# A fused mLSTM attention and gated FFN on one core: the first attention product moved to head pairs on two row groups, with split loads and a new order

## The chip, the cores and the metric

One core of a Trainium2 chip runs the whole program in one launch. The metric is the device time of one execution in microseconds (us), lower is better. The profile takes a single execution and gives its span, from the first to the last instruction it records.

## The reference

The input is q, k, v and an output gate of shape 4 x 8 x 768 x 40 (batch, heads, sequence, head size) with two gates per head and token. Attention is a recurrence with a stabilised exponential decay; its result, 320 wide per token, goes through a feed-forward network (FFN) with a convolution of three taps along the sequence.

```python
for t in range(S):
    m_new = np.maximum(f_gate[:, :, t] + m, i_gate[:, :, t])
    f_stab, i_stab = np.exp(f_gate[:, :, t] + m - m_new), np.exp(i_gate[:, :, t] - m_new)
    C = f_stab * C + i_stab * outer(vt, kt)
    n = f_stab * n + i_stab * kt
    y[:, :, t] = sigmoid(o_gate) * (C @ qt) / max(abs(n . qt), 1)
h = np.maximum(x @ w_in, 0)                  # 320 -> 1024
conv_out = sum(conv_w[k] * shifted(h, k) for k in range(3))
out = (h * sigmoid(conv_out)) @ w_out        # 1024 -> 320
```

## The kernel before, in words

**Tiles.** The sequence is cut into chunks of 128 tokens: 6 to a sequence, 24 in all, written s. Two neighbouring chunks make a unit u of 256 tokens (12 units); the FFN works on units, in eight blocks f of 128 hidden columns, which are treated in four pairs p.

**Attention of a chunk.** The gates are scanned on 32 rows (batch times head), and the decays reach the 128 rows of a chunk in two ways: for the first NP = 3 chunks by products on PE (ch_gpe, L402 to L409: a 512 column product with the triangle and four with a 32 row operand, columns of the identity against the 32 rows of Gt), later by a DMA that repeats rows of a DRAM tile (ch_loadw, L418), with a mask on POOL (L432) and an exponential on ACT (L439). The first product, S = k q for eight heads (ch_s, L455 to L466), comes in two jobs s0 and s1 of four heads. Its operands have 120 or 80 rows, three heads deep: kz holds each head's k in its own 40 rows with zeros in the rest, and q has the three heads stacked. DVE multiplies S by the decays (ch_p, L471). The product with v (ch_pv, L491) adds to the part that comes from the running state (ch_inter, L482). The state Cst is advanced by ch_u on PE and ch_state on DVE (L513, L515), and its masked copy cb for the next chunk's ch_inter is made by two products on POOL or DVE (ch_cb, L521 and L522). DVE then divides (ch_rden, then ch_num at L547, which reads pY in PSUM and writes x in SBUF), applies the output gate (ch_x, L554), and PE transposes (ch_t, L575) into X, split into a high and a low part.

**FFN of a unit.** Block f: eight products into ph (f_m1, L618), a relu on ACT (L628), the taps on ACT (L636) and DVE (L650). A pair of blocks then has a tanh on ACT (L654), a product on DVE (L658), and a split into gh on ACT (L213) and gl on POOL (L209). The second FFN product (f_m2, L681) is one job of six products per block: gh with both parts of w_out and gl with the high part, for two halves k of the tokens. Weights arrive as 64 bit numbers and are converted by integer operations on DVE (L330 to L343) and a split on ACT and POOL.

**Order.** All work is a table of jobs (`at`, L703) with engine costs (COST), the jobs each waits for, and a tie breaker z (OFF). A planner (`order`, L86) places them when the program is built, and each engine runs its instructions in that fixed order. Buffers are rings (BUFS): pY has one buffer, freed by the job num; the PSUM tag m has three. Where the planner sees a gap on PE ahead of the first m1, it puts in `warm` products on zeros (L358). In the trace an fp32 product shows as two MATMUL rows, an fp32r product (ph, po, the triangle, the transposes) as one.

## Time and profile before

| | |
|---|---|
| median of 3 runs | 345.4 us (345.09 to 349.81) |
| the profiled execution, device time | 344.72 us |
| its span | 342.6 us |
| PE, DVE, ACT, POOL busy | 328.7, 262.9, 236.3, 202.7 us |
| moved by DMA | 46.09 MB |

PE is TensorE's products and PEld its weight loads, which overlap them; DVE, ACT and POOL are VectorE, ScalarE and GpSimd; SP issues the DMAs. A busy share counts products that overlap only once, and the mean duration of a PE row contains the time that it takes to drain, so what a row of products costs is read from start to start. PEclk, the granted clock, is in tenths of full speed.

### The profile page before, as it was taken

The page shows a single profiled execution, that of the slowest core. Times are in us where ns is not written, and L with a number is a line of the kernel's source. Part 1 is how long each engine was busy: PE and PEld are TensorE (multiplying, and loading weights), DVE is VectorE, ACT ScalarE, POOL GpSimd, SP SyncE. Part 2 cuts the span into 40 slices and gives each one's busy share as a digit, 9 for nine tenths or more (in the row PEclk, how much of TensorE's full clock was granted, in tenths as well). Part 3 has the DMA queues.
Part 4 walks back from the last instruction along what each step waited for, and adds up shares of the span by engine and source line. Part 5 has one row for each costly group of instructions (what it writes and reads, how often), then busy time and mean ns, then how long its engine had stood idle before and what let it go on. Part 6 is the DMA issues. An engine that isn't in the chain of part 4 may idle for free.

```text
span 342.6 us, 7422 instructions
## 1 busy us (share of the span) xinstructions
PE 328.7 (96%) x2534; PEld 322.3 (94%) x2534; DVE 262.9 (77%) x598; ACT 236.3 (69%) x610; POOL 202.7 (59%) x310
## 2 busy tenths in 40 slices
PE   7699898998999999999999999999999999999995
PEld 7588898999999999999999999999999999999995
DVE  4897889999998987778489877676888768566750
ACT  2355747879988668896958786769685536577871
POOL 7369898869968647584745661746563234343341
PEclk9855599999999999999999999999999999999999
DMA  6887658686717466174315452654211001010111
GB/s 167 273 250 299 215 196 271 192 256 180 221 53 219 150 194 205 64 216 157 101 58 153 127 160 93 187 182 147 94 59 41 0 2 38 2 38 2 38 41 38
DMA packets 18575, 46.09 MB, mean 135 GB/s; under 512 B 2579, under 2 KB 6347, under 8 KB 18539
## 3 DMA queue, kind: packets, MB, share of 16 engines
q1 hardware_dynamic: 18068, 45.22, 42.4%
q8 instruction: 20, 0.33, 0.5%
q10 hardware_dynamic: 471, 0.41, 0.4%
q14 instruction: 16, 0.13, 0.1%
HBM read 41.49 MB, written 4.13 MB: 133 GB/s over the span
## 4 chain that ended last, share of the span: by engine, by line
PE 71%; DVE 11%; POOL 6%; ACT 4%; DMA 3%; issue 3%; SPq 0%; POOLq 0%; DVEq 0%; ACTq 0%
PE po L681 22%; PE ph L618 22%; PE pY L491 10%; PE pS L464 9%; PE pY L482 3%; PE pU L502 3%; PE pT L575 2%; DMA wraw<-in_w_in 1%; DVE cv L650 1%; DVE ph L650 1%; ACT w L439 1%; DMA w<-G_d 1%; PE pg L408 1%; POOL gl L209 1%; POOL w L432 1%
## 5 line engine op out<-in xcount | busy, mean ns | idle before, releaser
L209 POOL TENSOR_TENSOR gl<-cv,gh 128x512 fp32r<-128x512 f32 x48 | 62.5, 1302 | 47.4 <-ACT gh L213 40.7
L618 PE MATMUL ph<-X,wi_h 128*128 128x258 f32 x480 | 77.1, 290 | 2.2 <-DVE cv L650 1.5
L618 PEld LDWEIGHTS ph<-X,wi_h 128*128 128x128 f32 x480 | 64.6, 190 | 3.0 <-ACT ph L636 1.7
L681 PE MATMUL po<-wo_h,gh 128*128 128x320 f32 x192 | 61.5, 320 | 0.5 <-ACT ot L687 0.5
L439 ACT ACTIVATE w<-w,aT 128x128 f32<-128x128 f32 x168 | 55.1, 391 | 8.1 <-POOL w L432 8.1
L650 DVE SCALAR_TENSOR_TENSOR ph<-h,cw_sb,ph 128x256 f32<-128x256 f32 x96 | 46.1, 483 | 18.9 <-ACT ph L636 18.4
L681 PE MATMUL po<-wo_l,gh 128*128 128x320 f32 x192 | 59.3, 309 | 0.0
L681 PE MATMUL po<-wo_h,gl 128*128 128x320 f32 x192 | 59.3, 309 | 0.0
L464 PE MATMUL pS<-q,kz 120*128 120x128 f32 (+1 forms) x384 | 53.1, 287 | 4.2 <-DVE aT L306 3.1
L464 PEld LDWEIGHTS pS<-q,kz 120*128 120x128 f32 (+1 forms) x384 | 48.6, 199 | 4.6 <-DVE aT L306 3.2
L658 DVE SCALAR_TENSOR_TENSOR cv<-cv,h 128x512 f32<-128x512 f32 x48 | 40.4, 844 | 15.9 <-ACT cv L654 15.6
L628 ACT ACTIVATE h<-ph 128x258 f32<-128x258 f32 x96 | 36.5, 380 | 23.1 <-PE ph L618 21.2
L650 DVE SCALAR_TENSOR_TENSOR cv<-h,cw_sb,ph 128x256 f32<-128x256 f32 x96 | 45.1, 476 | 8.1 <-POOL gl L209 4.9
L618 PE MATMUL ph<-X,wi_l 128*128 128x258 f32 x288 | 50.3, 283 | 0.0
L491 PE MATMUL pY<-n,w 128*128 128x41 f32 x384 | 47.8, 282 | 0.0
L491 PEld LDWEIGHTS pY<-n,w 128*128 128x128 f32 x384 | 47.2, 197 | 0.2
L636 ACT ACTIVATE ph<-h,cw_sb 128x256 f32<-128x256 f32 x96 | 45.6, 475 | 1.9
L654 ACT ACTIVATE cv<-cv 128x512 f32<-128x512 f32 x48 | 30.1, 627 | 16.3 <-DVE cv L650 9.3
L618 PEld LDWEIGHTS ph<-X,wi_l 128*128 128x128 f32 x288 | 41.3, 190 | 0.0
L213 ACT ACTIVATE gh<-cv 128x512 fp32r<-128x512 f32 x48 | 30.0, 624 | 11.2 <-PE po L681 11.2
L681 PEld LDWEIGHTS po<-wo_h,gh 128*128 128x128 f32 x192 | 36.2, 188 | 0.7 <-ACT ot L687 0.7
L681 PEld LDWEIGHTS po<-wo_l,gh 128*128 128x128 f32 x192 | 36.2, 189 | 0.0
(84 smaller groups left out, 530.0 us busy)
## 6 DMA issues: line engine op xcount, KB each, us to landing
n<-in_nat SPq DMA_DIRECT2D x24, 484.0 KB
w<-G_d SPq DMA_DIRECT2D x21, 512.0 KB
q<-in_qT SPq DMA_DIRECT2D x12, 360.0 KB
out<-ot SPq DMA_DIRECT2D x24, 160.0 KB
wraw<-in_w_in SPq DMA_DIRECT2D x8, 384.0 KB
kz<-in_kT SPq DMA_DIRECT2D x24, 120.0 KB
eq<-E_d SPq DMA_DIRECT2D x24, 120.0 KB
wraw<-in_w_out SPq DMA_DIRECT2D x8, 320.0 KB
```

What stands on the lines that cost most here:

```text
L209: (nc.gpsimd if e == "POOL" else nc.vector).tensor_tensor(out=out, in0=in0, in1=in1, op=op)
L213: nc.scalar.activation(out, in_, AF.Copy)
L439: nc.scalar.activation(w[:, h, :], g, AF.Exp, bias=aT[:, c, b * 8 + h : b * 8 + h + 1])
L464: nc.tensor.matmul(pS[:, j, :], lhsT=lhsT, rhs=rhs, start=(j == 0), stop=(j == 3), skip_group_check=True)
L491: nc.tensor.matmul(pY[:, h * VW : (h + 1) * VW], lhsT=r["w"][:, n, :], rhs=v[:, DM + h * VW : DM + (h + 1) * VW], start=(c == 0 and n == 0 ...
L618: nc.tensor.matmul(ph, lhsT=a, rhs=b_, start=(i == 0), stop=(i == len(mm) - 1))
L628: nc.scalar.activation(hj, ph, AF.Relu)
L636: nc.scalar.activation(c, hk, AF.Copy, scale=wk)
L650: nc.vector.scalar_tensor_tensor(o, hk, wk, c, op0=ALU.mult, op1=ALU.add)
L654: nc.scalar.activation(cv, cv, AF.Tanh, scale=0.5)
L658: nc.vector.scalar_tensor_tensor(cv, cv, 1.0, h[:, :, 1 : 1 + UT], op0=ALU.add, op1=ALU.mult)
L681: nc.tensor.matmul(obuf[u][k], lhsT=a, rhs=b_, start=(f == 0 and i == 0), stop=(f == 7 and i == 2))
```

## The change

- **S in pairs.** ch_s becomes one job per chunk: eight products of 40 rows, which alternate between rows 0 to 39 and rows 64 to 103, each of the two into a bank of its own (two PSUM buffers of tag m at once). kz with its zeros goes away; k2 and q2 hold four heads side by side in each row group.
- **Loads.** k2 and q2 come by four DMAs of 40 rows per unit (kP, qP), with three buffers; the stacked q (still needed for the state's product) is a job of its own, ldq. Per unit 327,680 bytes more are moved.
- **Decays.** Gt becomes the first 32 rows of Gz, 128 rows with zeros below, and the products of ch_gpe use all 128 rows. The gates are scanned in four groups (1, 1, 2, 2 chunks) where there were three (1, 1, 4).
- **State copy.** ch_cb is three ACT instructions with a row scale; POOL and DVE have none of it. The mask shrinks to 120 x 3.
- **Division.** ch_num works in place in PSUM; ch_x reads PSUM, writes x, and now frees pY.
- **Second FFN product.** m2 (gh, four products) waits for gh; a new job m2l (gl, two products) waits for gl. The output copy and its DMA are a job for each half.
- **Order.** New OFF, COST and planner constants, and a table FIX that sets z and a release time for many jobs one by one. The warm products in the program go from 22 to 92.

```diff
-GS = ((0, 1), (1, 2), (2, 6))
+GS = ((0, 1), (1, 2), (2, 4), (4, 6))
...
-    wk={"POOL": 0.97, "DVE": 0.55}, u={"PE": 0.6}, state={"DVE": 0.72}, cb={"POOL": 1.0, "DVE": 0.5}, s0={"PE": 0.86}, s1={"PE": 0.86}, p0={"DVE": 0.61}, p1={"DVE": 0.61},
+    wk={"POOL": 0.97, "DVE": 0.55}, u={"PE": 0.6}, state={"DVE": 0.72}, cb={"ACT": 0.85}, s={"PE": 1.15}, p0={"DVE": 0.61}, p1={"DVE": 0.61},
...
+FIX = dict(
+    g0={0: (3413.08, 0)},
...
-ACT_W = dict(pv0=0.3, pv1=0.3, gpe=0.4)
-WARM = (6.0, 60.0, 16)
+ACT_W = dict(pv0=0.3, pv1=0.3, s=0.5, ta0=0.3, ta1=0.3, ta2=0.3, ta3=0.3, tw0=0.3, tw1=0.3, tw2=0.3, tw3=0.3)
+WARM = (5.0, 60.0, 9, 1.8, 0.22)
...
-    Gt = const.tile([32, S], F32, name="Gt")
+    Gz = const.tile([P, S], F32, name="Gz")
+    nc.vector.memset(Gz[32:64, :], 0.0)
+    nc.vector.memset(Gz[64:P, :], 0.0)
+    Gt = Gz[0:32, :]
...
-    def att_kz(u):
-        q = sb.tile([120, 3 * UT], F32, name="q", tag="q", bufs=3)
+    def att_kq(u):
+        r = units.setdefault(u, {})
+        for nm, src in (("k2", kP), ("q2", qP)):
+            r[nm] = t = sb.tile([104, 4 * UT], F32, name=nm, tag=nm, bufs=3)
+            for k in range(2):
+                nc.sync.dma_start(out=t[64 * k : 64 * k + D, :], in_=src[u, k * D : k * D + D, :])
+
+    def att_q(u):
+        q = units.setdefault(u, {})["q"] = sb.tile([120, 3 * UT], F32, name="q", tag="q", bufs=3)
         nc.sync.dma_start(out=q, in_=qT[u])
...
-            nc.tensor.matmul(p[:, j, :], lhsT=id_sb[0:32, r : r + 1].to_broadcast([32, P]), rhs=Gt[:, c * P : (c + 1) * P],
+            nc.tensor.matmul(p[:, j, :], lhsT=id_sb[:, r : r + 1].to_broadcast([P, P]), rhs=Gz[:, c * P : (c + 1) * P],
...
-    def ch_s(s, half):
+    def ch_s(s):
         u, tt = s // 2, (s % 2) * P
         r, ur = chunks[s], units[u]
-        pS = ps_m.tile([P, 4, P], F32, name="pS", tag="m")
+        for half in range(2):
+            r["s", half] = ps_m.tile([P, 4, P], F32, name=f"pS{half}", tag="m")
         for j in range(4):
-            n = 4 * half + j
-            g = n % 3
-            kk = 40 * GRP[g][1]
-            lhsT, rhs = ur["kz"][0:kk, n, tt : tt + P], ur["q"][0:kk, g * UT + tt : g * UT + tt + P]
-            nc.tensor.matmul(pS[:, j, :], lhsT=lhsT, rhs=rhs,
-                             start=(j == 0), stop=(j == 3), skip_group_check=True)
-        r["s", half] = pS
+            for half in range(2):
+                k, q = (ur[x][64 * half : 64 * half + D, j * UT + tt : j * UT + tt + P] for x in ("k2", "q2"))
+                nc.tensor.matmul(r["s", half][:, j, :], lhsT=k, rhs=q, start=(j == 0), stop=(j == 3), skip_group_check=True)
...
-    def ch_cb(e, s):
+    def ch_cb(s):
         cb = sb.tile([120, 3, 123], F32, name="cb", tag="cb")
-        mk3 = mk_sb.rearrange("p (g v) -> p g v", g=3)
-        tt(e, cb[:, 0:2, :], Cst[:, 0:2, :], mk3[:, 0:2, :], ALU.mult)
-        tt(e, cb[0:80, 2, 0:82], Cst[0:80, 2, 0:82], mk3[0:80, 2, 0:82], ALU.mult)
+        for j in range(3):
+            ng, sl = 3 if j < 2 else 2, slice(j * VW, (j + 1) * VW)
+            nc.scalar.activation(cb[:, 0:ng, sl], Cst[:, 0:ng, sl], AF.Copy, scale=mk_sb[:, j : j + 1])
...
-        xf = sb.tile([P, 3 * P], F32, name="x", tag="x")
-        x = xf[:, 0:DM].rearrange("p (h d) -> p h d", h=H)
-        nc.vector.tensor_tensor(x, y3[:, :, 0:D], r["rd"].unsqueeze(2).to_broadcast([P, H, D]), op=ALU.mult)
-        r["x"] = xf
+        y3 = r["y"].rearrange("p (h d) -> p h d", h=H)[:, :, 0:D]
+        nc.vector.tensor_tensor(y3, y3, r["rd"].unsqueeze(2).to_broadcast([P, H, D]), op=ALU.mult)
 
     def ch_x(s):
         r = chunks[s]
-        xf = r["x"]
-        o = r["n"][:, DM + H * VW :]
-        nc.vector.scalar_tensor_tensor(xf[:, 0:DM], o, 1.0, xf[:, 0:DM], op0=ALU.add, op1=ALU.mult)
+        xf = r["x"] = sb.tile([P, 3 * P], F32, name="x", tag="x")
+        x, o = (t.rearrange("p (h d) -> p h d", h=H) for t in (xf[:, 0:DM], r["n"][:, DM + H * VW :]))
+        y3 = r["y"].rearrange("p (h d) -> p h d", h=H)[:, :, 0:D]
+        nc.vector.scalar_tensor_tensor(x, o, 1.0, y3, op0=ALU.add, op1=ALU.mult)
...
-        at("inter", z, qe + [("cb", us - 1)] if c else [], ch_inter, s, ring="y", users=[("num", s), ("rd1", s)], cost=0.63 if c else 0.01)
+        at("inter", z, qe + [("cb", us - 1)] if c else [], ch_inter, s, ring="y", users=[("x", s)], cost=0.63 if c else 0.01)
...
-    def f_m2(u, f):
+    def f_m2(u, f, low):
         p, j = f // 2, f % 2
-        gh, gl = gbuf[u, p]
-        if f == 0:
+        g = gbuf[u, p][low]
+        if f == 0 and not low:
             obuf[u] = [ps_o.tile([P, DM], F32, name=f"po{k}", tag=f"o{k}") for k in range(2)]
+        ws = [wo_h[:, f, :]] if low else [wo_h[:, f, :], wo_l[:, f, :]]
         for k in range(2):
-            ks = slice(k * P, (k + 1) * P)
-            mm = ((gh[:, j, ks], wo_h[:, f, :]), (gh[:, j, ks], wo_l[:, f, :]), (gl[:, j, ks], wo_h[:, f, :]))
-            for i, (a, b_) in enumerate(mm):
-                nc.tensor.matmul(obuf[u][k], lhsT=a, rhs=b_, start=(f == 0 and i == 0), stop=(f == 7 and i == 2))
-
-    def f_out(e, u):
-        for k in range(2):
-            ot = sb.tile([P, DM], F32, name="ot", tag="ot", bufs=2)
-            if e == "ACT":
-                nc.scalar.activation(ot, obuf[u][k], AF.Copy, scale=0.5)
-            else:
-                nc.vector.tensor_scalar(ot, obuf[u][k], 0.5, None, op0=ALU.mult)
-            ots[u, k] = ot
-        del obuf[u]
-
-    def f_outd(u):
-        b, t0 = u // 3, (u % 3) * UT
-        for k in range(2):
-            ot = ots.pop((u, k))
-            nc.sync.dma_start(out=out[b, t0 + k * P : t0 + (k + 1) * P, :], in_=ot)
+            for i, w in enumerate(ws):
+                nc.tensor.matmul(obuf[u][k], lhsT=g[:, j, k * P : (k + 1) * P], rhs=w, start=(f == 0 and not low and i == 0), stop=(f == 7 and low == 1))
...
-            at("m2", n, [("gl", 4 * u + f // 2), ("wsl", 8 + f)] + ([("m2", n - 1)] if n else [(f"exp", 4 * NP - 1)] if NP else []) + ([("out", u - 1)] if u and not f else []), f_m2, u, f)
+            at("m2", n, [("gh", 4 * u + f // 2), ("wsl", 8 + f)] + ([("m2", n - 1)] if n else [(f"exp", 4 * NP - 1)] if NP else []) + ([(f"out{k}", u - 1) for k in range(2)] if u and not f else []), f_m2, u, f, 0)
+            at("m2l", n, [("gl", 4 * u + f // 2), ("m2", n)] + ([("m2l", n - 1)] if n else []), f_m2, u, f, 1)
```

**The order on PE in the second half.** Rows of TensorE around one chunk's S, before (pU: the state's update; po: second FFN product; ph: first):

```order
L618 MATMUL ph<-X,wi_l 128x258 x3
L502 MATMUL pU<-n,wk 120x123 x2
L502 MATMUL pU<-n,wk 80x82
L464 MATMUL pS<-q,kz_108 128x128 x8
L681 MATMUL po_3283<-wo_h,gh 128x320
L681 MATMUL po_3283<-wo_l,gh 128x320
L681 MATMUL po_3283<-wo_h,gl 128x320
```

and at the like place now (k and q with numbers are the tiles k2 and q2, which the list shortens):

```order
L609 MATMUL pU<-n,wk 80x82
L785 MATMUL po_3233<-wo_h,gl 128x320
L785 MATMUL po_3234<-wo_h,gl 128x320
L572 MATMUL pS_3409<-q_2683,k_2680 128x128
L572 MATMUL pS_3410<-q_2683,k_2680 128x128
L572 MATMUL pS_3409<-q_2683,k_2680 128x128
L572 MATMUL pS_3410<-q_2683,k_2680 128x128
L572 MATMUL pS_3409<-q_2683,k_2680 128x128
L572 MATMUL pS_3410<-q_2683,k_2680 128x128
L572 MATMUL pS_3409<-q_2683,k_2680 128x128
L572 MATMUL pS_3410<-q_2683,k_2680 128x128
L723 MATMUL ph<-X,wi_h 128x258 x5
```

Eight products in one row into one bank after another have become four pairs that alternate between two banks, and the gl products of po stand by themselves.

**The order on PE ahead of the first m1.** Before, after the last pg (decays) products of the start, with pt the transposes of the gates, pT those of x, and pw the warm products:

```order
L408 MATMUL pg_371<-Gt,id_sb 128x128 x4
L575 MATMUL pT<-id_sb,x 128x128 x3
L502 MATMUL pU<-n,wk 120x123 x2
L502 MATMUL pU<-n,wk 80x82
L464 MATMUL pS<-q,kz_107 128x128 x8
```

and now, at the third chunk's pg:

```order
L414 MATMUL pt<-id_sb,rst 128x32 x2
L472 MATMUL pw<-wz 128x128 x19
L609 MATMUL pU<-n,wk 120x123 x2
L609 MATMUL pU<-n,wk 80x82
L472 MATMUL pw<-wz 128x128 x3
L514 MATMUL pg_423<-tri 128x512
L517 MATMUL pg_423<-Gz,id_sb 128x128 x4
L472 MATMUL pw<-wz 128x128 x4
L680 MATMUL pT<-id_sb,x 128x128 x3
```

Warm products now stand between the real ones; 9 lead the program and 83 more stand ahead of the first m1, where there were 16 and 6.

**The order on DVE just ahead of the first tap.** Before (wf: weight conversion, Cst: state, ph: the first tap):

```order
L515 SCALAR_TENSOR_TENSOR Cst<-Cst,dcol,pU 80x82
L341 SCALAR_TENSOR_TENSOR wf<-wraw,wf 128x320
L547 TENSOR_TENSOR x<-pY,rd 128x320
L343 SCALAR_TENSOR_TENSOR wf<-wraw,wf 128x320 x2
L554 SCALAR_TENSOR_TENSOR x<-n,x 128x320
L650 SCALAR_TENSOR_TENSOR ph<-h,cw_sb,ph 128x256
```

and now:

```order
L444 TENSOR_SCALAR wmag<-wmag 128x384
L652 TENSOR_TENSOR pY<-pY,rd 128x8x40
L622 SCALAR_TENSOR_TENSOR Cst<-Cst,dcol,pU 120x123 x2
L622 SCALAR_TENSOR_TENSOR Cst<-Cst,dcol,pU 80x82
L659 SCALAR_TENSOR_TENSOR x<-n,pY 128x320
L453 TENSOR_SCALAR wf<-wmag 128x384
L755 SCALAR_TENSOR_TENSOR ph<-h,cw_sb,ph 128x256
```

Ahead of the first tap all eight blocks of w_in (384 columns) and two of w_out (320) were converted; now six of w_in are, and the first two steps of the seventh. The rest stands behind it.

More of the change, by code (lines that the diff above doesn't have):

```diff
@@ L73 @@
 LAG, PELAG = 0.035, 0.3
-SWAP = {'DVE': 2.13, 'POOL': -0.08, 'ACT': 0.51}
+SWAP = {'DVE': 15.43, 'POOL': 0.98, 'ACT': 0.06}
 DMALAG = (0.65, 0.7)
-ACT_W = dict(pv0=0.3, pv1=0.3, gpe=0.4)
-HAM = (3.4133, 0.37, 0.92)
-WARM = (6.0, 60.0, 16)
+ACT_W = dict(pv0=0.3, pv1=0.3, s=0.5, ta0=0.3, ta1=0.3, ta2=0.3, ta3=0.3, tw0=0.3, tw1=0.3, tw2=0.3, tw3=0.3)
+HAM = (3.4133, 0.4, 0.92, 0.5)
+WARM = (5.0, 60.0, 9, 1.8, 0.22)
 def holds(key, eng):
@@ L94, in order, with busy @@
     ready = {}
-    win, act = [0, False], {0: 1.5, 1: 2.73}
+    win, act = [0, False], {}
+    def busy(a, b, w):
+        while a < b:
+            k = int((a - HAM[3]) / HAM[0] + 1e-9)
+            c = min(b, HAM[3] + (k + 1) * HAM[0])
+            act[k] = act.get(k, 0.0) + (c - a) * w
+            if c <= a:
+                break
+            a = c
+    busy(WARM[3], FREE0["PE"], 1.0)
     queue = {e: [] for e in free}
@@ L163, in order @@
             if e == "PE":
-                while t >= (win[0] + 1) * HAM[0]:
+                while t >= HAM[3] + (win[0] + 1) * HAM[0]:
                     a = act.pop(win[0], 0.0) / HAM[0]
@@ L196, in tile_mlstm_ffn @@
 @with_exitstack
-def tile_mlstm_ffn(ctx, tc, fg, ig, qT, kT, nat, w_in, w_out, cw, msk, tr, out):
+def tile_mlstm_ffn(ctx, tc, fg, ig, qT, qP, kP, nat, w_in, w_out, cw, msk, tr, out):
     nc = tc.nc
@@ L700, in tile_mlstm_ffn, with f_out, f_outd, at @@
+    def f_out(e, u, k):
+        ot = ots[u, k] = sb.tile([P, DM], F32, name="ot", tag="ot", bufs=2)
+        if e == "ACT":
+            nc.scalar.activation(ot, obuf[u][k], AF.Copy, scale=0.5)
+        else:
+            nc.vector.tensor_scalar(ot, obuf[u][k], 0.5, None, op0=ALU.mult)
+    def f_outd(u, k):
+        t0 = (u % 3) * UT + k * P
+        nc.sync.dma_start(out=out[u // 3, t0 : t0 + P, :], in_=ots.pop((u, k)))
     jobs = {}
     seen = {}
-    def at(key, z, after, fn, *a, ring=None, users=(), cost=None):
+    def at(key, z, after, fn, *a, ring=None, users=(), users2=None, cost=None):
```

239 lines of the change are left out of this document (166 added, 73 removed).

## The prediction

> **What bounds the kernel now.** First the page of the profile: busy time, the span in slices, the chain that ended last.
>
> ```profile
> span 342.6 us, 7422 instructions
> ...
> PE 328.7 (96%) x2534; PEld 322.3 (94%) x2534; DVE 262.9 (77%) x598; ACT 236.3 (69%) x610; POOL 202.7 (59%) x310
> ...
> PE   7699898998999999999999999999999999999995
> ...
> DVE  4897889999998987778489877676888768566750
> ...
> PEclk9855599999999999999999999999999999999999
> ...
> PE 71%; DVE 11%; POOL 6%; ACT 4%; DMA 3%; issue 3%; SPq 0%; POOLq 0%; DVEq 0%; ACTq 0%
> ```
>
> PE is busy 96% of the span, and the chain lies on it for 71%, so work taken off PE should count. But PEclk shows 5 in slices two to five: there PE ran at half pace, and DVE was as full as PE up to the sixteenth slice or so. A mean over the span hides two stages, so the second view is busy time by stretch of the span.
>
> ```profile
> core 0: us, PE busy (x) PEld busy (x) DVE busy (x) ACT busy (x) POOL busy (x), PEclk, DMA share, GB/s
> 0.00:10.00 10.00, 8.19 (x43) 7.58 (x43) 4.47 (x16) 2.89 (x7) 6.11 (x13) 1.00 0.71 174
> 10.00:20.00 10.00, 6.93 (x37) 5.99 (x36) 9.57 (x12) 4.44 (x15) 5.37 (x7) 0.71 0.85 258
> 20.00:30.00 10.00, 10.00 (x45) 8.64 (x44) 7.58 (x17) 5.04 (x15) 8.00 (x14) 0.50 0.98 338
> 30.00:40.00 10.00, 8.91 (x38) 7.95 (x38) 9.57 (x20) 6.65 (x21) 8.21 (x12) 0.50 0.63 213
> 40.00:60.00 20.00, 18.49 (x156) 17.76 (x156) 17.68 (x44) 12.49 (x39) 18.84 (x31) 0.96 0.72 226
> 60.00:80.00 20.00, 19.11 (x162) 18.70 (x161) 19.48 (x46) 16.53 (x48) 15.14 (x22) 1.00 0.75 229
> 80.00:120.00 40.00, 39.30 (x334) 38.88 (x333) 38.03 (x96) 33.51 (x96) 31.44 (x51) 1.00 0.53 157
> 120.00:240.00 120.00, 119.71 (x971) 119.48 (x971) 89.79 (x210) 91.99 (x237) 69.55 (x115) 1.00 0.47 146
> 240.00:320.00 80.00, 79.66 (x638) 79.38 (x637) 57.92 (x131) 51.88 (x117) 33.16 (x44) 1.00 0.10 33
> 320.00:342.60 22.60, 18.42 (x130) 17.89 (x129) 8.81 (x16) 10.89 (x23) 6.84 (x6) 0.98 0.08 30
> ```
>
> From 120 us to 320 us PE is busy 199.37 of 200 us at full clock, while DVE has a quarter to spare: the **back** is PE's alone. What is left of PE after 320 is the tail behind its last product, which the change doesn't touch in length. Up to 120 us, the **front**, DVE idles 13.6 us in all (10 less 4.47, and so on down the column), 5.5 of it in the first ten; from 60 to 120 it is 96% busy (57.51 of 60). There PE and DVE go in step, and a cheaper S buys nothing unless DVE goes faster too. How much of S lies in each stage, in MATMUL rows, 16 to a chunk:
>
> ```profile
> core 0: us, PE busy (x) PEld busy (x), PEclk, DMA share, GB/s
> 0.00:60.00 60.00, 13.17 (x80) 11.96 (x80) 0.77 0.77 239
> 60.00:120.00 60.00, 12.78 (x96) 11.63 (x96) 1.00 0.60 181
> 120.00:342.60 222.60, 27.18 (x208) 24.96 (x208) 1.00 0.30 94
> ```
>
> Five chunks run their S by 60 us, six by 120, thirteen in the back.
>
> **The change part by part.** *S in the back.* The chain of waits, in order of time, gives starts, and so what a row of products costs:
>
> ```profile
> 212.98 1.82 PE pS L464 x16
> 215.13 1.79 PE pS L464 x16
> 216.92 1.76 PE po L681 x12
> ...
> 299.27 1.93 PE ph L618 x16
> ```
>
> Sixteen rows of S take 1.82 and 1.79 us, so a chunk's S costs 1.80 us, 0.11 a row. If the two row groups run side by side, eight rows' time is left: 0.90. The trace has no pair of row groups, but it has changes between 128 and 32 rows, which bound what going in and out costs:
>
> ```profile
> 8.02 0.48 PE L405 MATMUL pg<-tri 128*128 128x512 f32 x1
> 8.43 1.15 PE L408 MATMUL pg<-Gt,id_sb 32*128 32x128 f32 x8
> 9.51 0.51 PE L405 MATMUL pg<-tri 128*128 128x512 f32 x1
> ...
> 12.21 0.24 PE L300 MATMUL pt<-id_sb,rst 32*128 32x32 f32 x1
> 15.52 2.08 PE L464 MATMUL pS<-q,kz 120*128 120x128 f32 x8 [3.07 <-DVE aT L306]
> ```
>
> The triangle's product, 512 columns, takes from 8.02 to 8.43. A ph row with 258 columns takes 0.121 (1.93 over 16) and a po row with 320 takes 0.147 (1.76 over 12), that is 0.42 ns a column, so 512 columns should take 0.23: 0.18 is left over where 32 rows follow. The eight pg rows from 8.43 to 9.51 take 1.08 against 8 x 0.1125 = 0.90, again 0.18, where 128 rows follow. So a change of row groups costs 0.18, and a block with one in and one out 0.90 + 0.36 = 1.26. From below it is 0.90 (no price for the change), from above 1.80 + 0.36 = 2.16 (the pairs in fact one after the other, and the changes paid). I take 1.26, since both of its parts come from rows of such products. Thirteen chunks: 13 x 0.54 = **7.0 us less**; the bounds are 11.7 less and 4.7 more. The Trainium skill, TensorE: Matmul & The Clock Gate, in its section Part 3: Packing small matmuls, gives a measured 3.07 for four row tiles where four would be whole; an estimate from it, at that yield, is 1.80 / 1.54 = 1.17 for a block, and the sum would lose 8.2 instead; the trace of before has no such pair to hold against it.
>
> *The front.* Its eleven S blocks, the clock and the new order are worth what they take out of DVE's idle time. What DVE waited for between 4 and 120 us:
>
> ```profile
> DVE mt L246 <- DMA it<-in_ig: 3.7, 1, 3.7
> DVE rd L534 <- PE pY L491: 3.4, 4, 2.3
> ...
> DVE w L471 <- PE pS L464: 1.4, 2, 1.2
> ```
>
> It waited 3.4 and 1.4 us for PE's products: **4.8 us**, and I take these as the gain. The 3.7 us for the first gates stay, since the same DMA comes first. The most is all of DVE's idle time but these, 13.6 - 3.7 = 9.9; the least is nothing, if DMA or DVE's own work sets the pace as it did. DVE's work itself doesn't shrink: by the order lists two blocks of w_in and two of w_out move behind the first tap, which lets the FFN begin sooner but must be done before m2 can go through. So the start of m1 some microseconds before today's 60 us isn't a gain by itself. The two memsets of Gz fall into DVE's 3.7 us wait.
>
> *The clock.* PE sat idle from 12.45 to 15.52 for the copy aT, and from there eight rows of S take 2.08 where they take 0.90 in the back: half pace or less, until the clock is back at 0.96 for 40 to 60. Now fifteen warm products stand in that place, and pg uses 128 rows. At full clock the 166 warm rows ahead of m1 cost 166 x 0.1125 = 18.7 us of PE, which lie in PE's waits for DVE; that cover is there as long as DVE is the slower of the two.
>
> *DVE, ACT and POOL.* The groups by line and shape that the change touches:
>
> ```profile
> L439 ACT ACTIVATE w<-w,aT 128x128 f32<-128x128 f32 x168 | 55.1, 391 | 8.1 <-POOL w L432 8.1
> ...
> L209 POOL TENSOR_TENSOR cb<-Cst,mk_sb 120x246 f32<-120x246 f32 x20 | 15.1, 754 | 5.5 <-DVE Cst L513 5.0 <-DVE Cst L515 0.5
> L554 DVE SCALAR_TENSOR_TENSOR x<-n,x 128x320 f32<-128x320 f32 x24 | 14.7, 612 | 0.3
> ...
> L547 DVE TENSOR_TENSOR x<-pY,rd 128x320 f32<-128x320 f32 x24 | 11.7, 486 | 0.5
> ...
> L209 POOL TENSOR_TENSOR cb<-Cst,mk_sb 80x82 f32<-80x82 f32 x20 | 8.0, 400 | 0.0
> ...
> L213 ACT ACTIVATE x<-x 128x64 f32<-128x64 f32 x15 | 3.7, 250 | 5.9 <-DVE x L554 5.9
> ```
>
> ch_num writing PSUM, and ch_x reading it, I cost as ch_num's row now, 486 ns; ch_x then has 0.13 less than its mean of 612, at least nothing, and about a microsecond in the front, which the four weight conversions that come over from POOL use up. ch_cb leaves POOL, where it took 23.1 us, for ACT: three instructions each between the 0.25 of a 64 column copy and the 0.33 of an exponential (55.1 over 168), so 0.85 a chunk, 17 us over 20 chunks. From 120 to 240 ACT is busy 91.99 of 120; ten copies make it 100.5 of some 115, or 87%. Behind a waiting cb stand exponentials and relus, and PE's products with the state wait for cb itself. pY's one buffer is held for ch_x too, 0.49 us longer; between a chunk's last pv and the next chunk's first product into pY stand one or more m1 (0.96 each), which hide it. Without them it would be 13 x 0.49 = 6.4 us in the back. For all new waits together I add **1.0 us**, as the back's own idle is 0.63 now; nothing at best, 6 at worst.
>
> *DMA.* 12 x 0.328 = 3.9 MB more, 2.3 MB of it in the front (seven units), or 7 us at the 338 GB/s of 20 to 30 us. By the DMA column the engines are busy 82 of the first 120 us, so 38 are there for it. The first S needs 0.655 MB where it needed 0.696, as the stacked q now comes on its own. SP issues 193 DMAs where it issued 179, and none of its waits stands ahead of PE in the back. Uncovered, it is part of the least case of the front.
>
> *Second FFN product, output.* The count of products is the same; waits on gl are no part of PE's back, so m2l gains nothing there. Gates in four groups: the same columns, a few fixed costs, within the wait of PE. Nothing.
>
> **Sum.** 342.6 - 7.0 - 4.8 + 1.0 = 331.8 of span. The execution shown had 344.72 of device time, 2.1 above its span, and lies 0.7 under the median of the runs; so **333.9 us**, 3.1% under that execution.
>
> **Rivals.** *It all falls in place.* S at 0.90 and DVE's whole idle time gained: 342.6 - 11.7 - 9.9 + 2.1 = 323.1; half way from the forecast, about 328. For it: ch_x takes 612 ns on the mean where ch_num with as many elements takes 486, so something holds DVE up now and then; no row tells whether it is POOL, which loses 23 us. Against it: DVE at 96% with PE at 97%.
>
> *The pairs don't overlap.* Then the change doesn't do what it says: S stays at 1.80, or 2.16 with the changes: 342.6 - 4.8 + 1.0 + 2.1 = 340.9, up to 345.6. For it: weight loads take as long as the products (PEld is busy as PE is), and if two groups load through one path, nothing is won. Against it: no row shows two groups at once.
>
> *The clock falls anyway.* From 20 to 30 us PE was busy 10.00 of 10.00 and stayed at 0.50: busy alone doesn't bring the clock back, and 40 row pairs may count as little as the 32 row and 41 column products there. Then the 166 warm rows, in PE's fixed order, hold up the real ones: if half pace lasts the 27 us it did, PE loses 13.5 us, of which DVE's waits hide some; with no gain and 4 us lost in the front it is 342.6 + 4.0 - 7.0 + 1.0 + 2.1 = 342.7. The page of the skill just named says, in Part 1: The HAM clock gate, that a single busy window of some 3.4 us brings the full clock; by that rule the warm products make sure of it, and this rival is out, but the ten microseconds at 0.50 in the trace speak against the rule as it stands.
>
> *ACT holds up the state.* The slower side: at 87% a cb finds an instruction or two ahead of it, a pair of exponentials (0.65 us) and more, and PE's order is fixed, so each late cb stops PE. At 0.8 us for each of 20 chunks it is 16 us: 342.6 - 7.0 - 4.8 + 16 + 2.1 = 348.9. From 0.6 us a chunk it eats the whole gain. For it: ACT from 80 to 120 is already busy 33.51 of 40. Against it: cb took 1.15 us on POOL and had a queue there too.
>
> **How the numbers follow.** Forecast 0.68, all in place 0.10, no overlap 0.08, clock 0.07, ACT 0.07. A measurement of this kernel can tell about 2% from no change: faster is under 338.5, slower over 352.3. The forecast with its bounds lies under 338.5 nine times in ten (0.61), the better case always (0.10), a little of the others (0.01): faster 0.72. Most of the overlap and clock cases, a tenth of the forecast and a part of ACT's are within: 0.21. Slower 0.07. The range goes from 324.5, between the better case and the forecast's own low end, to 343.0, which takes in the clock case and half of the no overlap case.
>
> **What would show it.** S blocks of 1.1 to 1.3 us from start to start in the back, against 1.80; PEclk without the fives of 15 to 41 us; PE full from 120 us on; DVE still over 93% busy between 60 and 110 us; ACT in the high eighties in the middle, and PE waiting for cb less than 0.2 us a chunk. The prediction is wrong if S blocks stay near 1.8, if the warm products run at half pace, or if PE idles over 3 us after 120 us.

## The result, and the profile after

The changed kernel takes 358.04 us (median of three runs, 357.30 to 358.31), the kernel before 345.40: a ratio of 1.037, with an interval of 1.0355 to 1.039. Slower by 3.7%, where 3.3% faster was forecast, and far outside the range. A ratio leaves out executions more than 1.5% above the fastest of their kernel, so it needn't be the quotient of the medians beside it. The page of the profiled execution, whose device time is 358.31:

```profile
span 356.5 us, 7717 instructions
...
PE 335.9 (94%) x2674; PEld 322.5 (90%) x2674; DVE 252.0 (71%) x604; ACT 254.5 (71%) x686; POOL 172.4 (48%) x259
...
PE   5999899997779899999999998999999999999995
...
DVE  6435836997798998476885875984885984766570
...
PEclk9999969997889999999999999999999999999999
...
PE 62%; DVE 11%; DMA 10%; POOL 6%; ACT 4%; issue 4%; SPq 1%; ACTq 0%; POOLq 0%; DVEq 0%
```

The three fives of PEclk (slices three to five; slice two had an 8) are gone; there is one 6 at slice six and a dip at ten to twelve. The column doesn't show all of it: it has the full clock for the first 40 us, yet up to some 20 us PE's rows take twice their time, as the timeline below shows. DVE now has 4, 3, 5, 8 and 3 in slices two to six, where it was at 7 to 9, and DMA has a tenth of the chain where it had 3%. The same stretches as before:

```profile
core 0: us, PE busy (x) PEld busy (x) DVE busy (x) ACT busy (x) POOL busy (x), PEclk, DMA share, GB/s
0.00:10.00 10.00, 6.24 (x26) 5.86 (x27) 7.26 (x18) 2.57 (x5) 4.19 (x13) 1.00 0.78 210
10.00:20.00 10.00, 10.00 (x50) 8.81 (x49) 4.74 (x11) 4.29 (x15) 3.36 (x6) 1.00 0.69 190
20.00:30.00 10.00, 10.00 (x80) 9.34 (x78) 4.56 (x18) 4.60 (x16) 2.43 (x6) 1.00 0.79 228
30.00:40.00 10.00, 9.85 (x93) 9.49 (x93) 5.68 (x13) 3.05 (x8) 7.40 (x17) 1.00 0.52 158
40.00:60.00 20.00, 19.17 (x149) 18.45 (x150) 11.94 (x34) 11.83 (x38) 10.50 (x18) 0.83 0.94 263
60.00:80.00 20.00, 18.97 (x181) 17.75 (x180) 16.91 (x43) 17.06 (x54) 14.81 (x22) 1.00 0.82 276
80.00:120.00 40.00, 32.10 (x223) 29.46 (x222) 34.27 (x87) 32.72 (x89) 21.72 (x31) 0.87 0.62 190
120.00:240.00 120.00, 117.48 (x1003) 113.40 (x1002) 91.65 (x223) 96.71 (x272) 69.27 (x107) 1.00 0.52 158
240.00:320.00 80.00, 79.60 (x651) 78.15 (x650) 55.68 (x130) 59.15 (x146) 26.52 (x33) 1.00 0.14 46
320.00:356.50 36.50, 32.54 (x237) 31.79 (x235) 19.32 (x36) 22.55 (x50) 12.24 (x9) 0.98 0.08 28
```

PE is as busy as ever and DVE, which sets the pace of the front, is not: in the first 120 us it is busy 85.4 us where it was 106.4, so it idles 34.6 instead of 13.6. PE's busy time deceives, since warm products are in it (the page's group of pw has 184 rows). What counts is how many rows of real work lie behind at 120 us. The view of the stretch from 120 us on, tile by tile, has for before and after:

| rows left at 120 us | ph | po | pY | pU | pT | pS |
|---|---|---|---|---|---|---|
| before | 600 | 534 | 284 | 66 | 42 | 208 |
| after | 631 | 552 | 340 | 72 | 51 | 240 |

At 0.121 us for a row of ph, 0.147 for po and 0.12 for the others, the first five are 198.14 us before and 213.06 after: 14.9 more. S itself, in the back, by the chain of waits:

```profile
223.73 1.09 PE pS L572 x16
224.82 2.11 PE ph L723 x16
...
319.07 1.93 PE ph L723 x16
```

Sixteen rows of S take 1.09 us, and the ph block behind them 2.11 where another takes 1.93. So a chunk costs 1.09 + 0.18 = 1.27, where it cost 1.80.

**The account in the prediction's own terms.** S in the back: fifteen chunks are left, 15 x 0.53 = 8.0 us gained. The front: 14.9 us of other rows and two chunks of S (3.6 at the old price) lie behind, 18.5 lost. The rest, 3.4, is a remainder and not a row: 342.6 - 8.0 + 18.5 + 3.4 = 356.5, the span. Of it, 2.1 us are new waits, since PE's idle time behind 120 us grew by that much (from 0.63 to 2.92 up to 320 us, from 4.18 to 3.96 behind); 1.3 is not placed. The loss comes from the first 120 us; the experiments ask what makes it.

What DVE waited for there, after:

```profile
DVE aT L420 <- PE pt L414: 10.4, 3, 5.2
DVE rd L641 <- PE pY L597: 7.4, 3, 4.2
DVE Cst L622 <- POOL eq L320: 4.1, 1, 4.1
```

10.4 and 7.4 us, with 0.9 of w for pS 18.7, are waits for PE's products, four times the 4.8 that the forecast had hoped to remove. PE's timeline shows why pt and pY are late:

```profile
15.33 2.93 PE L472 MATMUL pw<-wz 128*128 128x128 f32 x12
18.18 0.31 PE L414 MATMUL pt<-id_sb,it 32*128 32x32 f32 x1
18.43 3.30 PE L472 MATMUL pw<-wz 128*128 128x128 f32 x18
...
44.55 3.56 PE L597 MATMUL pY<-n,w 128*128 128x41 f32 x16
47.91 3.66 PE L472 MATMUL pw<-wz 128*128 128x128 f32 x16
```

Twelve warm rows, 2.85 us from start to start where full pace would be 1.35, stand ahead of a transposition for which DVE waits until 18.53; sixteen rows of pY take 3.56 us at half pace where they take 1.92 at full. And DMA in the chain of that stretch, beside the issue of the last of the eight w_in loads, which came at 24.91 us before:

```profile
18.37 5.89 DMA q<-in_qP
24.27 5.74 DMA k<-in_kP
...
35.47 5.62 DMA wraw<-in_w_in
```

```profile
62.17 0.36 SPq L435 DMA_DIRECT2D wraw<-in_w_in  x1
```

These loads aren't late by their bytes alone. From 10 to 40 us DMA's share is 0.69, 0.79 and 0.52 by stretches of ten, where it was 0.85, 0.98 and 0.63. The w_in load of 35.47 stands on SP behind one of the stacked q, which waited 5.6 us there until POOL had multiplied eq by q, at 35.07. POOL had waited 7.0 and 3.4 us for wT, which ACT makes from transpositions (pt) that PE did at 23.59 and 28.56. So late products and late loads are links of one chain.

```profile
POOL wk L320 <- ACT wT L422: 10.4, 2, 7.0
...
35.09 0.33 SPq L488 DMA_DIRECT2D q<-in_qT  x1
```

Four suspects follow, with letters where the expectations of the first runs have them: the warm products that hold up real ones (A), the pairs' bytes and late loads (B), the clock that falls where PE has less to do (C), and the order.

### The profile page after: what moved, and what is told of

It reads as the page before. It is cut to its first block, busy times and chain, and to the rows that moved or that the text cites. A ratio compares the mean times of both kernels' runs of the same rounds, so it can differ in the third digit from the quotient of the medians.

```text
span 356.5 us, 7717 instructions
## 1 busy us (share of the span) xinstructions
PE 335.9 (94%) x2674; PEld 322.5 (90%) x2674; DVE 252.0 (71%) x604; ACT 254.5 (71%) x686; POOL 172.4 (48%) x259
## 4 chain that ended last, share of the span: by engine, by line
PE 62%; DVE 11%; DMA 10%; POOL 6%; ACT 4%; issue 4%; SPq 1%; ACTq 0%; POOLq 0%; DVEq 0%
PE po L785 20%; PE ph L723 20%; PE pY L597 8%; PE pS L572 4%; PE pY L588 3%; PE pw L472 3%; DMA wraw<-in_w_out 2%; DVE ph L755 2%; PE pU L609 2%; ACT w L548 2%; DMA ltm<-in_tr 2%; DMA q<-in_qP 2%; DMA eq<-E_d 2%; DMA k<-in_kP 2%; DMA wraw<-in_w_in 2%
## 5 line engine op out<-in xcount | busy, mean ns | idle before, releaser
L723 PE MATMUL ph<-X,wi_h 128*128 128x258 f32 x480 | 78.8, 295 | 8.0 <-DVE cv L755 5.8
L723 PEld LDWEIGHTS ph<-X,wi_h 128*128 128x128 f32 x480 | 65.5, 192 | 12.7 <-ACT ph L741 3.2
L548 ACT ACTIVATE w<-w,aT 128x128 f32<-128x128 f32 x168 | 56.4, 392 | 4.6 <-POOL w L541 4.6
L785 PE MATMUL po<-wo_h,gh 128*128 128x320 f32 x192 | 58.5, 316 | 1.1 <-ACT wo_h L324 1.0
L785 PE MATMUL po<-wo_l,gh 128*128 128x320 f32 x192 | 57.5, 312 | 0.5 <-POOL wo_l L320 0.5
L597 PE MATMUL pY<-n,w 128*128 128x41 f32 x384 | 48.8, 287 | 0.6 <-DVE w L577 0.6
L763 DVE SCALAR_TENSOR_TENSOR cv<-cv,h 128x512 f32<-128x512 f32 x48 | 38.7, 807 | 12.1 <-ACT cv L759 12.0
L541 POOL TENSOR_SCALAR_AFFINE_SELECT w<-w 128x1024 f32<-128x1024 f32 x21 | 24.6, 1170 | 31.3 <-DMA w<-G_d 18.2
L785 PE MATMUL po<-wo_h,gl 128*128 128x320 f32 x192 | 35.5, 315 | 1.0 <-POOL gl L320 1.0
L577 DVE TENSOR_TENSOR w<-w,pS 128x512 f32<-128x512 f32 x48 | 31.6, 679 | 1.6 <-PE pS L572 1.3
```

Of the source, the lines that this page charges most:

```text
L548: nc.scalar.activation(w[:, h, :], g, AF.Exp, bias=aT[:, c, b * 8 + h : b * 8 + h + 1])
L577: nc.vector.tensor_tensor(w, w, r["s", half], op=ALU.mult)
L597: nc.tensor.matmul(pY[:, h * VW : (h + 1) * VW], lhsT=r["w"][:, n, :], rhs=v[:, DM + h * VW : DM + (h + 1) * VW], start=(c == 0 and n == 0 ...
L723: nc.tensor.matmul(ph, lhsT=a, rhs=b_, start=(i == 0), stop=(i == len(mm) - 1))
L763: nc.vector.scalar_tensor_tensor(cv, cv, 1.0, h[:, :, 1 : 1 + UT], op0=ALU.add, op1=ALU.mult)
L785: nc.tensor.matmul(obuf[u][k], lhsT=g[:, j, k * P : (k + 1) * P], rhs=w, start=(f == 0 and not low and i == 0), stop=(f == 7 and low == 1))
```

## The experiments

Each is compared with the kernel before, run on the same chip; ratios have their 95% interval.

**Warm products (three runs).** The changed kernel, in the loop that emits the jobs:

```diff
         if e[0] == "warm":
-            warm(e[1])
             continue
```

> The changed kernel with the same order on every engine, but without the 83 warm products between the real ones ahead of the first m1 (the nine at the start stay). Theory A, the warm products in PE's fixed order hold up the transposes, scores and state products that DVE waits for (it waited 10.4 us for the transposed gates and 6.3 for pv): the time falls by 10 to 17 us, to 341 to 348, even if the clock stays low longer. Theory B, late DMAs set the front: it falls by less than 3. Theory C, the clock is what matters and the warm products keep it: it rises by 3 to 10, to 361 to 368.

366.4 us, 1.055 (1.046 to 1.064): slower than with them (1.037). In the execution profiled (366.8 us) the clock is at half from 40 to 60 us throughout:

```profile
40.00:60.00 20.00, 15.94 (x83) 14.75 (x83) 9.97 (x27) 11.00 (x35) 8.87 (x15) 0.50 0.78 212
```

With the nine warm products at the start made sixteen beside it (`warm(16)` for `warm(WARM[2])`):

> As the kernel without warm products in the gaps, but with sixteen warm products at the start in place of nine, as before the change. If the half pace between 8 and 19 us costs the front (theory A's second part), it is 2 to 5 us under the kernel without gap products; if the clock at the start is only incidental, within 1 us of it.

364.9 us, 1.059 (1.052 to 1.066), the same within the intervals. With half of them (`warm(e[1] // 2)`):

> The changed kernel with its order, and half of the warm products in each gap (0 of them gave 366 us, all of them 358). If the warm products mainly hold up the real ones: 350 to 356. If they mainly keep the clock: 359 to 364, on the line between the two.

359.0 us, 1.042 (1.038 to 1.047), at the lower edge of the second range: half do nearly as well as all. They hold up some work: without them the transposition of 18.18 us comes at 16.01. And they keep some clock: without them it is 0.59 from 30 to 40 us, where it was 1.00. The two about balance, so A is not the net cause: taking all of them away makes it worse.

**Pairs and loads alone.** The kernel before, its planner and numbers, with S in pairs and the split loads (ch_s, att_kq and att_q of the change; an S job of 1.1 us for two of 0.86). The order is then planned anew.

> The kernel before with S in pairs and the split loads alone; its planner, costs but for S, start and warm products as before the change. If the pairs are worth in the back what the rows of the changed kernel say (1.09 for 1.80, thirteen chunks) and nothing in the front: 9 us less, 334 to 339. If what was lost comes with the pairs or their loads: 345 or more.

358.0 us, 1.039 (1.033 to 1.045), the whole of what the change costs. DMA has 18% of the chain.

So what pairs and loads cost is as much as all parts together. That the others (zeros under the decays, the state's copies on ACT, po in two jobs, new numbers) are worth nothing doesn't follow, as the two orders differ.

**Where.** Before, with pairs and their loads from the seventh unit on only, in the zeroed tiles' own memory:

```diff
+        if u >= 6:
+            f = kz.rearrange("p h t -> p (h t)")
+            r.update(q=q, k2=f[:, 0 : 4 * UT], q2=f[:, 4 * UT : 8 * UT])
...
+        if u >= 6:
+            at("s", z, sd, ch_s2, s, ring="m", users=[("p0", s)], users2=[("p1", s)])
```

> The kernel before, with pairs and split loads only from the seventh unit on (twelve of 24 chunks, all in the back); the first six units load and compute S as before, so the first 100 us have the old bytes and the old products. The later half is planned anew with the cheaper S. Loads theory and clock theory alike: 336 to 341 (345 less 12 blocks of 0.53, with the following ph block's 0.18 paid, and 0 to 3 us of new waits). Order theory: 345 to 350, since the order changes here too.

341.8 us, just over the range, 0.993 (0.991 to 0.995): the only one here that is faster than both kernels, by 0.7% against before, which is little, with an interval clear of 1. Of the 12 x 0.53 = 6.4 us that S gives, 2.5 are left in the medians; where the others go is open. From the fourth unit on:

> As the run with pairs from the seventh unit on (341.8 us), but from the fourth unit on: six chunks more, which run between 55 and 120 us, have the pairs and their loads. If the front loses to the pairs' bytes and to TensorE's missing work only in its first 60 us: 336 to 340 (six blocks of 0.53 less). If it loses as long as DVE sets the pace, to 115 us: 342 to 349.

350.7 us, over both ranges, 1.017 (1.015 to 1.019): six chunks more, which run between 55 and 120 us, turn 0.7% faster into 1.7% slower. The two, seventh unit first:

```profile
60.00:120.00 60.00, 58.17 (x492) 57.36 (x490) 57.28 (x142) 50.42 (x145) 46.88 (x73) 1.00 0.60 192
```

```profile
60.00:120.00 60.00, 49.95 (x439) 47.38 (x440) 57.87 (x141) 47.34 (x137) 43.75 (x69) 0.97 0.68 213
```

DVE is as full in both; PE does 439 rows instead of 492 and idles 10 us instead of 2. The front is sensitive to its end, and not in its first 60 us alone.

**Bytes.** Before with its own S and order, each unit also loading the paired q into a tile that nothing reads:

```diff
+        q2 = sb.tile([104, 4 * UT], F32, name="q2", tag="q2", bufs=2)
+        for k in range(2):
+            nc.sync.dma_start(out=q2[64 * k : 64 * k + D, :], in_=qP[u, k * D : k * D + D, :])
```

> The kernel before, S and every engine's order as they were, but each unit also loads the two halves of the paired q (0.33 MB more, two DMAs on SP, into a tile that nothing reads). It has the pairs' load on DMA and nothing else. Loads theory (more bytes in the one queue make the weights and decays of the first 60 us late, and the engines stand in their fixed order): 353 to 358 us, as the kernel with pairs and loads alone took 358. Clock theory (the cheaper S leaves TensorE with too little to do in the front, and the clock falls): 345 to 347. Order theory (the order that the planner makes with a cheaper S is what costs): 345 to 347.

348.7 us, 1.013 (1.009 to 1.018), 4.5 us: a third of the loss, between the two ranges. The wait that grows most is DVE's for a weight block (5.8 us here, 1.6 before), whose load stands behind the added ones:

```profile
DVE wmag L330 <- ACT wmag L326: 5.8, 2, 3.9
```

The other way round, the changed kernel with k and q loaded once, so that S of every unit is made from the first unit's:

```diff
+            if u:
+                r[nm] = units[0][nm]
+                continue
```

> The changed kernel with k2 and q2 loaded for the first unit only and used for all units (S of the other units is computed from the first unit's q and k); order and everything else as they are, 7.2 MB and 44 DMAs less. Theory B, the new loads make the weights and decays late: the time falls by 8 to 15 us, to 343 to 350. Theory A, the warm products hold up the front: it falls by less than 4.

353.0 us, 1.024 (1.020 to 1.029), between the two ranges, and the same edit in the kernel before with pairs:

> The kernel before with S in pairs, in the order of the earlier run that took 358 us, but the paired k and q are loaded for the first unit only and used for all: every other unit's S is made from the first unit's q and k, so the output is not the reference's. 7.2 MB and 44 DMAs less than that run, 3.6 MB less than before. Loads theory: 338 to 346. Clock theory: 350 to 357, the granted clock still under 0.9 in several stretches of the first 80 us. Order theory: 350 to 358.

351.9 us, 1.023 (1.019 to 1.028), in the range of those who hold that bytes are not all. Against their own bases, 1.037 and 1.039, bytes are worth 4.4 and 5.4 us, with 3.4 and 3.3 MB less moved than before. So of B the bytes stand, as about a third of the loss. The late loads are not settled by it: with the bytes gone, the changed kernel's last w_in load is issued at 54.62 us instead of 62.17 (24.91 before), and SP still waits 12.3 and 6.7 us for POOL in the first 70.

**TensorE's missing work.** Before with nothing added, and half of S's products left out in the first twelve chunks:

```diff
-        for j in range(4):
+        nj = 2 if s < 12 else 4
+        for j in range(nj):
```

> The kernel before in its own order and with its own loads, but in the first twelve chunks half of S's products are left out (two of each four heads take the S of the other two): eight rows instead of sixteen, 0.9 us for a chunk where it took 1.8, all at 120 or 80 rows, no pairs. It does strictly less work than before, 10.8 us of TensorE. Theory 1 (TensorE is left without work at its waits in the front, a wait grows long enough for the clock to fall, and what follows runs at half pace): no gain or a loss, 345 to 356. Theory 2 (it is the form of the pairs, 40 rows each, that does not keep the clock): 338 to 344. If TensorE's time in the front counts as such: 335 to 338.

349.7 us, 1.015 (1.013 to 1.017). 10.8 us of work less makes the kernel 5 us slower, with the same order and bytes. The clock comes back later and falls once more:

```profile
40.00:60.00 20.00, 18.58 (x115) 18.04 (x115) 12.92 (x35) 9.98 (x31) 16.96 (x29) 0.68 0.54 173
...
80.00:100.00 20.00, 18.04 (x127) 17.88 (x128) 17.47 (x49) 17.06 (x49) 17.05 (x25) 0.83 0.56 171
```

and DVE waits 8.7 us for pY where it waited 3.4. How such a fall goes is seen best in the run with pairs loaded once (351.9 us); stretches of 3 us with PE's busy time and rows, the granted clock, DMA's share and GB/s, then PE's timeline:

```profile
114.00:117.00 3.00, 0.92 (x8) 0.91 0.24 35
117.00:120.00 3.00, 1.90 (x9) 0.50 1.00 336
120.00:123.00 3.00, 3.00 (x22) 0.50 0.53 204
123.00:126.00 3.00, 3.00 (x15) 0.50 0.01 3
126.00:129.00 3.00, 3.00 (x12) 0.50 0.66 171
129.00:132.00 3.00, 2.85 (x18) 0.81 0.42 171
```

```profile
118.11 1.55 PE L481 MATMUL pY<-cb,eq 120*128 120x123 f32 x6 [3.09 <-DVE x L546]
...
120.22 2.08 PE L465 MATMUL pS<-q,k 40*128 40x128 f32 x16
122.23 3.63 PE L490 MATMUL pY<-n,w 128*128 128x41 f32 x16
125.67 0.61 PE L680 MATMUL po<-wo_h,gh 128*128 128x320 f32 x1
...
130.36 0.31 PE L680 MATMUL po<-wo_l,gh 128*128 128x320 f32 x1
```

PE waits 3.09 us for DVE, from 115.02 to 118.11, and by stretches of 1 us the clock goes down between 116 and 117 (0.73) and is then at half. S with 40 rows and pY with 41 columns keep PE full without lifting it; it is back just behind 130 us, after 3.3 us of po, 128 rows by 320 columns, and 1.1 of pY with 123. So half pace lasts some 13 us. A wait of 3 us isn't needed: in the run with half of S the second fall, at some 83 us, follows a wait of 2.21, and in the changed kernel the clock goes down between 44 and 45 us (0.75) behind a wait of 0.83. Nor are few rows or columns all that keeps it down: from 7.97 to 13.32 us the changed kernel's PE is full with pg, 128 rows by 512 and 128 columns, and two short transpositions, and its rows go at half pace throughout. What lifts the clock stays open. The Trainium skill, TensorE: Matmul & The Clock Gate, in HAM oscillation, warns of idle gaps over some 3.4 us; the falls here came at 3.09 and less. By its Part 1: The HAM clock gate, a single busy window of some 3.4 us ends the half pace; here it lasted through nine us of full PE, from 120 to 129.

Is it the time or the form? Pairs' loads, before's order, both halves of S on rows 0 to 39 (`ur[x][0:D, ...]`), so one after the other:

> Pairs' loads and before's order as in the run that took 361 us, but both halves of S read rows 0 to 39, so the sixteen rows run one after the other (1.8 us a chunk); the second half of the heads gets the first half's S. Theory 1 (the missing time): 347 to 351, as with the loads alone. Theory 2 (the form with 40 rows does not keep the clock): 355 to 362. The S block itself should show 1.8 us.

388.2 us, 1.115 (1.105 to 1.125), worse than either theory. In the execution profiled (393.0 us) the clock is low for 120 us:

```profile
0.00:60.00 60.00, 48.84 (x226) 44.09 (x227) 35.37 (x83) 25.11 (x74) 33.99 (x59) 0.60 0.69 215
60.00:120.00 60.00, 58.54 (x377) 56.07 (x377) 44.72 (x107) 37.03 (x106) 37.21 (x58) 0.77 0.63 178
```

PE is busy 58.54 of 60 us at a mean of 0.77, where 120 and 80 rows in the same time had 57.22 (the run with more loads) and 58.41 (before), both at 1.00. But the places of the S blocks differ too, and an S block on one row group takes 1.98 us at full clock (from 271.72 and from 320.92 us), more than the 1.80 of before. So the form is suggested and not isolated. The 1.98 settles something else: it is 1.80 and a change of row groups, 0.18, and the pairs' 1.09 is then 0.91 and 0.18, half the rows' time.

Filling: four zero products of 128 rows ahead of each of the first twelve S blocks, in the pairs with the old order:

```diff
+        if s < 12:
+            for i in range(4):
+                nc.tensor.matmul(r["s", 0][:, 0, :], lhsT=wz, rhs=wz, start=True, stop=True, skip_group_check=True)
```

> The run that took 361 us (pairs, their loads, before's order) with four products of 128 rows and 128 columns of zeros ahead of each S block of the first twelve chunks: eight more rows, 0.9 us, so that TensorE has 2.0 us a chunk where the pairs leave 1.1 and before had 1.8. Both theories of the clock: faster than without the filling, 343 to 352. If the clock is not the cause, the filling is 10.8 us of work more: 361 to 370.

359.9 us, between the ranges, 1.044 (1.040 to 1.047), against 1.048 (1.042 to 1.054) without: no difference is resolved. And in the changed kernel with k and q loaded once:

> The changed kernel with the paired k and q loaded for the first unit only (353.0 us; S of other units from the first unit's q and k) and four products of zeros, 128 rows by 128 columns, ahead of each S block of the first twelve chunks. If the missing work of TensorE and the clock that falls with it are the rest of the loss: 345 to 351. If not, the filling is only more work: 354 to 362.

359.1 us, 1.040 (1.033 to 1.046), slower than without (1.024). Here the theory fails. The clock is full from 20 to 60 us, the bytes are gone, and DVE still idles 17 of these 40 us:

```profile
20.00:40.00 20.00, 20.00 (x175) 18.97 (x174) 10.42 (x30) 8.59 (x27) 11.38 (x24) 1.00 0.53 161
40.00:60.00 20.00, 19.95 (x189) 19.19 (x189) 12.49 (x34) 13.32 (x43) 9.88 (x16) 1.00 0.90 284
```

So here neither clock nor bytes make the most of DVE's waits: in the first 120 us it waits 8.4 us for pt and 4.4 for pY, where the changed kernel has 10.4 and 7.4. Rows that hold the clock stand in PE's fixed order like any others. What this run leaves as it was is that order, and weights nearly as late (the last w_in load is issued at 55.27 us).

**The order.** Pairs and loads in before's order, both halves where the first stood (`if first: return` in ch_s):

> The kernel before with S in pairs and the split loads, but every engine's order is that of before: both halves of S stand where the first stood, the four loads and the stacked q where the old four DMAs stood. Loads theory: 352 to 358, like the planned order. Clock theory: 350 to 356. Order theory: 333 to 339, that is 345 less some 0.6 us for each chunk's S in the back and nothing lost in front.

361.0 us, over all three ranges, 1.048 (1.042 to 1.054): the new order isn't the whole cause. But part of this is the old order's own cost in the back, as the run with pairs from the seventh unit on shows when it keeps the old order:

> Pairs and their loads from the seventh unit on, as in the run of 341.8 us, but every engine keeps the order of before, both halves of S standing where the first stood. The front is the same in both. If the order matters little: 341 to 344. If pairs in an order that is made for two single halves make TensorE wait in the back (it needs two free PSUM buffers at once and stands an S block ahead): 348 to 356. Then the 361 us of the pairs in the old order are in part this, and not the front.

348.2 us, 1.011 (1.009 to 1.012), 6 us over the planned one (341.8) with a like front. PE waits there for what an S block that stands early needs, a buffer of tag m, which the state's product pU holds until DVE has read it into Cst:

```profile
PE pS L488 <- DVE Cst L537: 2.7, 5, 0.8
```

The changed kernel with the first six units as before:

> The changed kernel with its own planner and numbers, but the first six units (twelve chunks) load k and make S as the kernel before did; the pairs and their loads begin with the seventh unit. If the pairs and their loads in the front are what the change loses: 340 to 348. If the other parts (the decays over 128 rows, the state's copies on ACT, the product in two jobs, the new order) lose: 353 to 360.

373.9 us, 1.083 (1.078 to 1.088), outside both ranges. Its planner's table of places was made for other durations, and the order that comes out is a new one; it says nothing of the other parts. Late weights alone, in the kernel before:

```diff
         jobs["wld", i]["z"] = WL[i]
+        jobs["wld", i]["rel"] = {1: 14.3, 2: 17.1, ..., 8: 62.2, 9: 66.5, ..., 16: 103.8}.get(i, 0.0)
```

> The kernel before with S, loads and tiles as they were; only the loads of the sixteen weight blocks are released to the planner at the times at which the changed kernel's SP issued them (the eight w_in blocks between 14 and 62 us where before they came between 5 and 25, the eight w_out blocks between 67 and 104 where it was 34 to 77). Its orders follow from that. If late weights, whose conversion DVE then has to do when it is full anyway, are the change's loss in the front: 353 to 360. If it is TensorE's late products alone: 344 to 349.

360.6 us, 1.043 (1.038 to 1.048), just over the first range: loads at about the changed kernel's times, in an order planned around them, cost as much as the change and more. And the table left out of the changed kernel (`FIX = {}`), which brings the loads forward (the last w_in is issued at 49 us instead of 62, still 24 behind before's):

> The changed kernel without its table of fixed places and release times (FIX is empty), so that its planner orders by the other numbers alone: all eight w_in loads then stand ahead of the fourth unit's k and q on SP, and five blocks are converted on DVE ahead of the first rd. Late weights theory: 345 to 353. If TensorE's late products are the loss: 356 to 368.

362.2 us, 1.049 (1.043 to 1.055), not faster. Its clock is low instead, and DVE idles 14 of the 40 us from 20 on (18 in the changed kernel, 5 before):

```profile
20.00:40.00 20.00, 15.23 (x93) 14.38 (x94) 9.55 (x16) 9.99 (x32) 12.18 (x20) 0.76 0.75 212
40.00:60.00 20.00, 16.49 (x92) 14.90 (x91) 16.58 (x41) 10.67 (x31) 12.02 (x20) 0.56 0.87 273
```

Late weights, with an order planned around them, suffice for such a loss; that they are what causes it in the changed kernel isn't shown. They aren't needed for one either: the pairs in before's order had their last w_in load issued at 30.23 us, 5 behind before's, and took 361.0 us.

## Why the prediction was wrong

**S in the back: right.** 1.26 a chunk was forecast, in bounds of 0.90 to 2.16; 1.09 with 0.18 behind it came. The pairs do run side by side, and the price of the change between row groups, taken from pg and the triangle, holds to 0.01, on the way in (1.98 on one row group) and on the way out (2.11 for 1.93). The gain is 8.0 instead of 7.0 since two chunks more lay in the back. The estimate of 1.17 from the Trainium skill's table of row tiles (TensorE: Matmul & The Clock Gate, Part 3: Packing small matmuls) lies 0.08 over the pairs alone and 0.10 under what they cost with the block behind them.

**The front: this step failed.** The prediction put it as a gain of 4.8 us, DVE's waits for PE, with "the least is nothing, if DMA or DVE's own work sets the pace as it did". It came to a loss of 18.5. DVE's work didn't grow; its idle time did, from 13.6 to 34.6 us. The bound was wrong because it treated the front as a sum of busy times, in which a cheaper part can at worst be useless. It is a chain of waits in fixed orders, and each of three changes to the kernel before costs time there: 0.33 MB more a unit 4.5 us, 10.8 us less work for PE 5, weights about as late as the change has them 16 (this last in an order of its own). They can't be added up: the change costs 13.

**DMA: failed with it.** "the engines are busy 82 of the first 120 us, so 38 are there for it" counted the engines' time, and the same bytes added to the kernel before cost 4.5 us. In the changed kernel the engines are less full from 10 to 40 us than they were (fuller only from 40 to 60, 0.94 for 0.72), and yet q, k and a w_in block hold up the chain for some 5.7 us each: what came late was also the issue on SP, which stands in a fixed order and waits for other engines, 5.6 us for POOL ahead of the w_in load of 35.47. The 4.1 us that DVE waits for eq come by the same POOL, which had waited for transpositions.

**The clock: half right.** (The fives of PEclk before are in slices three to five, not two to five as the prediction reads them.) Half pace from 20 to 41 us did go, but up to some 20 us the rows, the warm ones too, ran at half pace, which the prediction had named as a sign of being wrong, and the clock fell elsewhere (0.83 from 40 to 60, 0.87 from 80 to 120). That the warm rows "lie in PE's waits for DVE; that cover is there as long as DVE is the slower" failed: 10.4 us of DVE's waits are for transpositions that stand in that order. The rival with the falling clock named both mechanisms and gave 342.7, with 4 us lost in front; the size was the error. Still, by the column the mean clock of the first 120 us was no lower than before:

```profile
0.00:120.00 120.00, 106.33 (x791) 99.16 (x792) 85.37 (x218) 76.12 (x221) 64.42 (x111) 0.93 0.73 219
```

against

```profile
0.00:120.00 120.00, 110.92 (x803) 105.50 (x803) 106.38 (x244) 81.55 (x236) 93.12 (x146) 0.89 0.69 210
```

The column has 1.00 where the rows went at half pace, up to some 20.3 us now and 6.7 before; with 0.50 put there, an estimate, the means are some 0.85 now and 0.86 before. So a lower clock on the whole isn't the loss. What half pace costs where DVE waits for it wasn't measured by itself.

**New waits: 2.1 us where 1.0 was forecast**, or 3.4 with the part not placed, in bounds of 0 to 6. PE idles 2.92 us from 120 to 320 us where it idled 0.63. ACT is at 96.71 of 120 us, 81%, not in the high eighties, and no wait for cb shows among PE's waits in the back: that rival (348.9) came nearest in time and was not what happened.

**What stays open** is how the 18.5 us of the front divide in the changed kernel. Bytes are some 4.5 of them, in three frames, though in two of these 7.2 MB were taken away where the change adds 3.9. For the rest, neither warm products (none, half, all), nor a held clock, nor the table of places gave a faster kernel, and the runs that bring back the old loads and S there change the order with them. No run undoes the gates' four groups or pg over 128 rows alone, which stand ahead of the late transpositions.

## What to carry to other kernels

That a cheaper step is at worst useless holds only where times add up; where engines stand in fixed orders and one queue feeds them, ask of each change what comes later behind it, and let the bound of a stage that is not understood reach below nothing. Price a change for the stage that its engine bounds and keep it out of the others: the pairs win 0.7% when only the last twelve chunks have them, and lose 3.9% when all have. Read an engine's idle time and rows done by a given moment, not its busy time, where filler work counts as busy.
